# New durations for matmuls, and a margin for the banks of the row maxima, in a hand-planned instruction order (attention and bilinear feed-forward on one core)

## The chip, the cores and the metric

The kernel runs on one core of a Trainium2 chip. The metric is device time in microseconds (us) of one execution; the time given for a kernel is the median of its runs. The core's engines run side by side, each in the order in which its instructions were written: TensorE (PE in the profile, with its weight loads apart as PEld), VectorE (DVE), ScalarE (ACT), GpSimd (POOL), and the queue of SyncE (SP), which here issues most DMA transfers. They wait for one another only through semaphores.

## What is computed

```python
xn = _layernorm(x)                          # x: 1 x 2048 x 576
q, k, v = split((xn @ wqkv), H=32, Dh=18)
p  = softmax(q k^T * 18 ** -0.5)            # 32 heads, 2048 x 2048 each
s  = concat_heads(p v) @ wo
h  = (xn @ w_gate) * (xn @ w_up)            # 2048 x 4608
g  = silu(h @ w_down)                       # 2048 x 576
return x + s * g
```

Everything is float32. The two branches, attention `s` and the feed-forward (GLU) `g`, need only `xn`, and so they can run at the same time.

## The kernel before

**Three parts.** A prologue (about the first 195 us of the profiled execution) normalises x, makes q, k and v and writes them to DRAM. The main phase runs attention and the feed-forward together. An end part multiplies by `wo`, gates and stores.

**Two streams on TensorE.** A contraction in the main phase is cut to 64 rows, so a matmul uses half of the array's rows: rows 0 to 63 or rows 64 to 127. Stream `r = 0` is the sequence of matmuls on the lower half, `r = 1` that on the upper one, and two matmuls of different streams overlap. There are two lengths: 512 columns (`LONG`: the up and gate projections at L678, and both kinds of scores) and 288 columns (`SHORT`: the down projection at L720). The product of probabilities and values (`pv_group`, L639) uses all rows and so needs both streams to stop; such a pause is called a visit (`visit`), and one visit takes as a rule 7 tiles of 128 keys.

**The feed-forward** goes in 72 units. In each unit either stream makes two accumulations of 27 LONG matmuls (stream 0 the up projection, stream 1 the gate) and four of 12 SHORT ones. ACT copies the up result out (L683), DVE multiplies gate with up (L690), DVE adds each down result to its sums (`acc`, L748).

**Attention** computes the scores twice. An `a` item (`a_item`, L596 and L598) is a LONG matmul of scores for 128 queries and 512 keys and a maximum over its 512 columns on DVE (`mx`). When the 64 items of a head are done, `max_fold` and `max_rows` turn the maxima into two extra rows of the operands (`pair`). A `b` item (`b_item`, L628 and L630) is the same product transposed with the maximum already taken off, and an exponential on ACT (`pt`). There are 32 x 64 = 2048 items of each kind. In almost all of the main phase `a` items go on stream 0 and `b` items on stream 1. Four finished `b` items of one tile of keys are due for a visit.

**Banks.** PSUM has two banks for `a` results, two for `b` results, and four (`g`) that the up, gate, down and value products share. An `a` matmul must wait until DVE has read the maximum of the `a` item two before it.

**The planner.** `order()` (L1097 on) writes out the whole instruction order of the main phase before anything runs. It keeps a model of the time: `clk[r]` is the moment at which stream r can start its next matmul; `issue(r, length)` advances it by `length`; `engine(eng, start, taken)` keeps when DVE, ACT and POOL are next free; `banks[tag]` holds when each bank can be written again; `moved()` is the DMA queue. At each step the stream that is behind gets its next instruction: a score item if its bank is free by the model (`at <= clk[r]`) and its goal has come (`goal <= clk[r]`), else the next feed-forward matmul. Goals (`a_goal`, `b_goal`) spread the score items evenly over `span`, the planned length of the phase, which is worked out from LONG, SHORT and the length of the visits. The goals of the `a` items run ahead of an even spread by `SOONER` = 10 us at the end, and `b` item i has the goal of `a` item i + 88. `late()` holds an `a` item back when a feed-forward accumulation is about to end and needs DVE; it does so no longer when the item is 4 us behind its goal. For an `a` item the model gives DVE 0.60 us after the matmul's 0.456 us, adds 0.095 us (`TAIL`) and `EARLY` = 0.17 us, and then counts the bank as free.

The model's numbers change nothing but the order: which instruction stands before which on TensorE, and through it on the other engines. What is computed, how many instructions there are and what each costs stay as they are. Whatever the model says, the semaphores keep an instruction from running too early.

Of the kernel before, what the change touches and what calls it, by code (L numbers as in the profile page):

```python
# [40 lines left out]
def kernel(  # L41
# [536 lines left out]
    with ExitStack() as mid:  # L578
# [9 lines left out]
        def a_item(h, i, r=0):  # L588

            t, c = divmod(i, 4)  # L590
            if i == 0:
                mx[h] = gp.tile([128, NT, 4], FT, name="mx", bufs=1)
            q, k = (pairs[h % 2], ring) if r else (ring, pairs[h % 2])
            p = bank("a", 2)
            rows = slice(64 * r, 64 * r + 64)
            nc.tensor.matmul(p, q[rows, t * 128:(t + 1) * 128], k[rows, c * 512:(c + 1) * 512],  # L596
                             start=True, stop=True)
            nc.vector.tensor_reduce(mx[h][:, t, c:c + 1], p, axis=AX.X, op=OP.max)  # L598
# [3 lines left out]
        def max_fold(h):  # L602
            ms[h] = mp.tile([128, NT], FT, name="m", bufs=1)
            nc.vector.tensor_reduce(ms[h], mx.pop(h), axis=AX.X, op=OP.max)

        def max_rows(h):
            m = ms.pop(h)
            mm = mp.tile([128, 2, NT], FR, name="mm", bufs=1)
            mt = mp.tile([128, 32], FT, name="mt", bufs=1)
            nc.vector.tensor_scalar(mm[:, 0, :], m, -1.0, None, op0=OP.mult)  # L610
            nc.vector.scalar_tensor_tensor(mm[:, 1, :], m, -1.0, mm[:, 0, :].bitcast(FT),
                                           op0=OP.mult, op1=OP.subtract)
            nc.vector.transpose(mt, mm.rearrange("p a t -> p (a t)").bitcast(FT))  # L613
            for r in (64, 0) if h == H - 1 else (64,):
                q = ring if r == 0 else pairs[h % 2]
                for g in range(4):
                    rows = q[r + R:r + R + 2, :].rearrange("j (t g i) -> j g t i", g=4, i=32)[:, g].bitcast(FT)
                    nc.gpsimd.dma_start(rows, mt[32 * g:32 * g + 32, :])  # L618
# [224 lines left out]
            xi[t] = fin["ep"].tile([128, D], FT, name="xi", bufs=8)  # L843
            nc.sync.dma_start(xi[t], x2[rows, :])

        LONG, SHORT = 0.2335, 0.1335

        def stream(r):

# [38 lines left out]
        N = 64  # L888
        TOTAL = H * N
        LEAD, MOST = 24, 40  # L890
        EARLY = 0.17
        PACE, SKEW, PULL, FIRST, ROWS = 1.005, 3.0, 3.0, 2.0, 6.0
        slots, gone = [0, 0], [0.0, 0.0]
        clk, free = [0.0, 0.0], {"DVE": 0.0, "ACT": 0.0, "POOL": 0.0}
# [2 lines left out]
        banks = {"a": [0.0] * 2, "b": [0.0] * 2, "g": [0.0] * 4}  # L897
        turn = {"a": 0, "b": 0}

        def next_free(tag):  # L900
            if tag == "g":
                return min(banks["g"])
            return banks[tag][turn[tag] % len(banks[tag])]

        def engine(eng, start, taken):
            free[eng] = max(free[eng], start) + taken
            return free[eng] + TAIL[eng]

        def issue(r, length):

            at = issued[0] = max(clk[r], issued[0])
            clk[r] = at + length + (0.11 if fresh[r] else 0.0)
            fresh[r] = False
            return at + (0.456 if length == LONG else 0.356)
# [34 lines left out]
        def feed(r, h, i):  # L949

            if i == 0:
                if h:
                    stacks.append((load_ring, (r, h, 1)))
                if h + 1 < H and (r or h):
                    stacks.append((load_pair, (r, h + 1)))
            if i == 32 and h + 1 < H:
                stacks.append((load_ring, (r, h + 1, 0)))
            for at, want in ((10, (load_ring, (r, h, 1))), (48, (load_pair, (r, h + 1))), (52, (load_ring, (r, h + 1, 0)))):
                if i == at and want in stacks:
                    stacks.remove(want)  # L960
                    send(want, max(clk))

        def a_next(r=0):
            nonlocal na
            h, i = divmod(na, N)
            feed(0, h, i)
            a_item(h, i, r)
            slot = turn["a"] % 2
            turn["a"] += 1
            banks["a"][slot] = engine("DVE", issue(r, LONG), 0.60) + EARLY  # L970
            na += 1
            if i == N - 1:
                max_fold(h)
                max_rows(h)
                rows_done[h] = engine("DVE", 0.0, 0.85) + ROWS
# [5 lines left out]
        def b_next(r=1):  # L981
# [8 lines left out]
            end = engine("ACT", issue(r, LONG), 0.495)  # L990
            banks["b"][slot] = end + EARLY
            nb += 1
# [36 lines left out]
        def visit(now):  # L1029
# [4 lines left out]
            if due:  # L1034
                now = max(now, next_free("g") - EARLY + 0.03)
            for h, t, at in due:
# [5 lines left out]
            for h in sorted({h for h, _, _ in due[:many]}):  # L1042
                ts = [t for g, t, _ in due[:many] if g == h]
                now = max(now, next_free("g") - EARLY + 0.03) + 0.859 * len(ts)
                k = banks["g"].index(next_free("g"))
                pv_group(h, ts, k)
                end = engine("DVE", now + 0.25, 0.60) if ts[0] else engine("ACT", max(now + 0.25, shown[0]), 0.495)
                banks["g"][k] = end + EARLY
                if ts[-1] == NT - 1:
# [47 lines left out]
        def order():  # L1097
# [5 lines left out]
            while any(heads) or na < TOTAL or nb < TOTAL or due:  # L1103
# [20 lines left out]
                if r == 0 and (na < TOTAL or nb < TOTAL - N) or r == 1 and nb == 0 and na < N:  # L1124
                    at, goal, score, can = next_free("a"), a_goal(na) + lean, a_next, na < TOTAL and na < nb + N + MOST and stacked(0, na)
                    can = can and not late(goal, r)
                else:
                    at, goal, score, can = next_free("b"), b_goal(nb) + lean, b_next, b_ready(r)
# [9 lines left out]
                elif op is not None:  # L1138
# [8 lines left out]
                    if end:  # L1147
                        done = engine(end[0], lands, end[1])
                        banks["g"][slots[r]] = done + EARLY
                        if kind == "d":  # L1150
# [148 lines left out]
```

## Time and profile before

| | |
|---|---|
| median of 3 runs | 2575.25 us (2573.8 to 2578.24) |
| the profiled execution | 2576.35 us, of which the span is 2574.6 us |
| main phase, first up or gate matmul to the last visit's start | 194.8 to 2499.56 us |
| TensorE clock granted over the span | 1.000 |
| PE, DVE, ACT, POOL busy (share of the span) | 99%, 74%, 57%, 23% |

The span runs from the first to the last instruction; the 1.75 us beside it lie before and after. Busy time on PE is the time in which at least one matmul is on record as running. As two streams overlap and the ends of matmuls are modelled, a busy PE can still be losing time: whether it does is seen from the distance between the starts of one stream's matmuls.

### The profile page before, as it was taken

The page shows a single profiled execution, that of the slowest core. Times are in us where ns is not written, and L with a number is a line of the kernel's source. Part 1 is how long each engine was busy: PE and PEld are TensorE (multiplying, and loading weights), DVE is VectorE, ACT ScalarE, POOL GpSimd, SP SyncE. Part 2 cuts the span into 40 slices and gives each one's busy share as a digit, 9 for nine tenths or more (in the row PEclk, how much of TensorE's full clock was granted, in tenths as well). Part 3 has the DMA queues.
Part 4 walks back from the last instruction along what each step waited for, and adds up shares of the span by engine and source line. Part 5 has one row for each costly group of instructions (what it writes and reads, how often), then busy time and mean ns, then how long its engine had stood idle before and what let it go on. Part 6 is the DMA issues. An engine that isn't in the chain of part 4 may idle for free.

```text
span 2574.6 us, 59106 instructions
## 1 busy us (share of the span) xinstructions
PE 2558.4 (99%) x24360; PEld 2080.9 (81%) x24360; DVE 1917.3 (74%) x3377; ACT 1458.4 (57%) x2688; POOL 594.3 (23%) x663
## 2 busy tenths in 40 slices
PE   8999999999999999999999999999999999999999
PEld 7899887778878778877877788877787888887779
DVE  6209777778778888877788888877788888777527
ACT  5222666666655555655555565655555665555561
POOL 3214434434421111111111112111111211111125
PEclk9999999999999999999999999999999999999999
DMA  7799988887785666665686656656686666665567
GB/s 245 234 281 275 273 228 232 225 222 218 220 202 180 179 181 178 171 183 153 179 196 177 172 161 191 178 157 177 169 198 156 177 187 174 174 178 166 155 182 254
DMA packets 195897, 504.57 MB, mean 196 GB/s; under 512 B 58112, under 2 KB 116352, under 8 KB 156588
## 3 DMA queue, kind: packets, MB, share of 16 engines
q1 hardware_dynamic: 185676, 489.05, 67.9%
q0 software_dynamic: 9952, 11.74, 1.7%
q8 instruction: 192, 3.15, 0.6%
q14 instruction: 77, 0.63, 0.1%
HBM read 312.21 MB, written 107.61 MB: 163 GB/s over the span
## 4 chain that ended last, share of the span: by engine, by line
PE 98%; DVE 1%; DMA 1%; ACT 0%; issue 0%; SPq 0%
PE pg L678 35%; PE pg L639 17%; PE pg L720 16%; PE pa L596 11%; PE pb L628 9%; PE pg L402 2%; PE pa L348 2%; PE pb L348 2%; PE pg L1229 1%; PE pa L1229 1%; PE pb L1229 1%; DMA xc<-sx 0%; DMA xin<-in_A_x_dram 0%; PE pg L334 0%; DVE mx L598 0%; DVE xcx L338 0%
## 5 line engine op out<-in xcount | busy, mean ns | idle before, releaser
L598 DVE TENSOR_REDUCE mx<-pa 128x1 f32<-128x512 f32 x2048 | 1361.8, 685 | 150.2 <-PE pa L596 67.4
L630 ACT ACTIVATE pt<-pb 128x512 f32<-128x512 f32 x2048 | 1155.0, 598 | 549.0 <-PE pb L628 464.7
L678 PE MATMUL pg<-xc,wgu 64*128 64x512 f32 x7776 | 1381.0, 389 | 1.5 <-DMA xc<-sx 1.5
L678 PEld LDWEIGHTS pg<-xc,wgu 64*128 64x128 f32 x7776 | 1032.3, 184 | 54.7 <-DMA xc<-sx 3.1
L628 PE MATMUL pb<-pair,ring 64*128 64x512 f32 x2006 | 783.8, 397 | 0.5 <-ACT us L683 0.5
L596 PE MATMUL pa<-pair,ring 64*128 64x512 f32 x2001 | 781.1, 396 | 0.4 <-DVE mx L598 0.4
L720 PE MATMUL pg<-wd,hs 64*128 64x288 f32 x3408 | 531.3, 292 | 1.2 <-DVE acc L748 1.2
L720 PE MATMUL pg<-wd,hx 64*128 64x288 f32 x3408 | 524.6, 292 | 0.0
L720 PEld LDWEIGHTS pg<-wd,hs 64*128 64x128 f32 x3408 | 468.3, 185 | 6.6 <-DVE acc L748 1.9
L720 PEld LDWEIGHTS pg<-wd,hx 64*128 64x128 f32 x3408 | 462.7, 185 | 3.6 <-DMA hx<-hs 0.5
L639 PE MATMUL pg<-pt,vt 128*32 128x512 f32 x4096 | 454.8, 594 | 0.0
L694 POOL TENSOR_TENSOR hs<-us,hs 128x512 fp32r<-128x512 f32 x144 | 186.1, 1292 | 1120.3 <-ACT hs L693 1101.8
L596 PEld LDWEIGHTS pa<-pair,ring 64*128 64x128 f32 x2001 | 362.6, 184 | 92.0 <-issue 47.8
L628 PEld LDWEIGHTS pb<-pair,ring 64*128 64x128 f32 x2006 | 364.0, 184 | 11.3 <-ACT pt L630 1.4
L639 PEld LDWEIGHTS pg<-pt,vt 128*32 128x32 f32 x4096 | 125.5, 110 | 283.8 <-issue 280.7
L645 DVE TENSOR_TENSOR oc<-oc,pg 128x512 f32<-128x512 f32 x69 | 47.5, 688 | 319.2 <-PE pg L639 319.0
L748 DVE TENSOR_TENSOR acc<-acc,pg 128x288 f32<-128x288 f32 x544 | 234.6, 445 | 26.7 <-PE pg L720 24.0
L693 ACT ACTIVATE hs<-us 128x512 fp32r<-128x512 f32 x144 | 91.0, 632 | 155.8 <-DVE us L690 151.7
L659 POOL DMA_DIRECT2D sot<-oc x124 | 64.0, 523 | 327.7 <-DVE oc L656 325.4
L618 POOL DMA_DIRECT2D pair<-mt x128 | 78.0, 615 | 225.2 <-DVE mt L613 218.6
L643 ACT ACTIVATE oc<-pg 128x512 f32<-128x512 f32 x32 | 19.2, 599 | 189.3 <-PE pg L639 189.3
L194 POOL TENSOR_TENSOR wgu<-wraw,wgu 128x384 fp32r<-128x384 f32 x108 | 108.4, 1017 | 68.2 <-ACT wgu L193 47.8
(141 smaller groups left out, 1381.9 us busy)
## 6 DMA issues: line engine op xcount, KB each, us to landing
wgu<-swg SPq DMA_DIRECT2D x102, 1152.0 KB
hx<-hs SPq DMA_DIRECT2D x142, 512.0 KB
wd<-swd SPq DMA_DIRECT2D x50, 1152.0 KB
swg<-wgu SPq DMA_DIRECT2D x36, 1152.0 KB
pair<-sqk SPq DMA_DIRECT2D x192, 144.0 KB
ring<-sqk SPq DMA_DIRECT2D x384, 72.0 KB
swd<-wd SPq DMA_DIRECT2D x18, 1152.0 KB
sqk<-hl SPq DMA_DIRECT2D x32, 512.0 KB
```

Of the source, the lines that this page charges most:

```text
L194: nc.gpsimd.tensor_tensor(w[:, 9 + b:12 + b, :], raw[:, b:b + 3, :], w[:, b:b + 3, :].bitcast(FT), op=OP.subtract)
L348: nc.tensor.matmul(p, wq[b, a], xcs[c][:, e, :], start=n == 0, stop=n == len(PAIRS) - 1)
L596: nc.tensor.matmul(p, q[rows, t * 128:(t + 1) * 128], k[rows, c * 512:(c + 1) * 512], start=True, stop=True)
L598: nc.vector.tensor_reduce(mx[h][:, t, c:c + 1], p, axis=AX.X, op=OP.max)
L628: nc.tensor.matmul(p, k[rows, t * 128:(t + 1) * 128], q[rows, c * 512:(c + 1) * 512], start=True, stop=True)
L630: nc.scalar.activation(pt[t, c], p, AF.Exp, scale=scale)
L639: nc.tensor.matmul(p[32 * c:32 * c + 32, :], vt[h // 2][:, t, 6 * (h % 2):6 * (h % 2) + 32], pt[t, c], start=t == ts[0], stop=t == ts[-1])
L678: nc.tensor.matmul(ps, gw[n][half[r], a, :], xg[i][half[r], e, :], start=k == 0, stop=k == len(TERMS) - 1)
L693: nc.scalar.activation(hj[:, 0, :], h32, AF.Copy)
L694: nc.gpsimd.tensor_tensor(hj[:, 1, :], h32, hj[:, 0, :].bitcast(FT), op=OP.subtract)
L720: nc.tensor.matmul(ps[:, 0:HALF], (hx if k else hs)[u][half[r], j, a, s * 128:(s + 1) * 128], dw[u][half[r], k, j, e, :], start=n == 0, st ...
L748: nc.vector.tensor_tensor(a, a, ps[:, 0:HALF], op=OP.add)
```

## The change

Three numbers of the model change, all in the scope of the planner:

```diff
-        LONG, SHORT = 0.2335, 0.1335
+        LONG, SHORT = 0.2285, 0.1325
...
-        EARLY = 0.17
+        EARLY, LOAD = 0.17, 0.10
...
-            banks["a"][slot] = engine("DVE", issue(r, LONG), 0.60) + EARLY
+            banks["a"][slot] = engine("DVE", issue(r, LONG), 0.60) + EARLY + LOAD
```

A LONG matmul is counted 5 ns shorter, a SHORT one 1 ns shorter. `LONG` and `SHORT` also enter `part`, and with it `span` and `pace`, so the goals in model time move closer together. A bank of the maxima is taken to be usable 0.10 us later than before. The durations of DVE, ACT, POOL, DMA transfers and visits in the model stay.

## The prediction

> **What bounds the kernel now.** I read the page first (engines, then the chain that ended last), then the groups by line of the main phase, then two single stretches between visits.
>
> ```profile
> span 2574.6 us, 59106 instructions
> ...
> PE 2558.4 (99%) x24360; PEld 2080.9 (81%) x24360; DVE 1917.3 (74%) x3377; ACT 1458.4 (57%) x2688; POOL 594.3 (23%) x663
> ...
> PE 98%; DVE 1%; DMA 1%; ACT 0%; issue 0%; SPq 0%
> ```
>
> TensorE is 98% of the chain. The change neither adds nor removes an instruction, so the only time it can win is what TensorE loses between its matmuls. That amount comes from the groups by line of the main phase (window 194.7 to 2499.7):
>
> ```profile
> L678 PE MATMUL pg<-xc,wgu 64*128 64x512 f32 x7776 | 1381.0, 389 | 1.5 <-DMA xc<-sx 1.5
> L628 PE MATMUL pb<-pair,ring 64*128 64x512 f32 x2006 | 783.8, 397 | 0.5 <-ACT us L683 0.5
> L596 PE MATMUL pa<-pair,ring 64*128 64x512 f32 x2001 | 781.1, 396 | 0.4 <-DVE mx L598 0.4
> L720 PE MATMUL pg<-wd,hs 64*128 64x288 f32 x3408 | 531.3, 292 | 1.2 <-DVE acc L748 1.2
> L720 PE MATMUL pg<-wd,hx 64*128 64x288 f32 x3408 | 524.6, 292 | 0.0
> L639 PE MATMUL pg<-pt,vt 128*32 128x512 f32 x4068 | 451.8, 594 | 0.0
> L596 PE MATMUL pa<-ring,pair 64*128 64x512 f32 x47 | 18.7, 401 | 0.0
> L628 PE MATMUL pb<-ring,pair 64*128 64x512 f32 x42 | 16.9, 402 | 0.0
> ```
>
> and from the ends of the phase and one visit (one line's instructions, the timeline, the chain by pieces):
>
> ```profile
> L678 PE MATMUL pg<-xc,wgu x7776: 383/386/501, 194.8 to 2490.4; 64*128 64x512 f32 x200
> ...
> L596 PE MATMUL pa<-pair,ring x2001: 383/390/502, 200.6 to 2417.7; 64*128 64x512 f32 x182
> ...
> 2499.13 0.49 PE L628 MATMUL pb<-pair,ring 64*128 64x512 f32 x1
> 2499.56 2.78 PE L639 MATMUL pg<-pt,vt 128*32 128x512 f32 x24
> ...
> 358.37 6.15 PE pg L639 x56
> ...
> 387.91 6.15 PE pg L639 x56
> ```
>
> LONG matmuls: 7776 + 2006 + 2001 + 47 + 42 = 11872, or 5936 a stream. SHORT: 6816, or 3408 a stream. Visits: 4064 records before the last one (4068 less the 4 at its start) at 6.15 us for 56 give 446 us. With the new constants the work is 5936 x 0.2285 + 3408 x 0.1325 + 446 = 1356 + 452 + 446 = 2254 us; the phase took 2499.56 - 194.8 = 2305. So 51 us lie beyond the counted work, over some 74 stretches 0.69 us each. Not all of it can go. The stretch from 364.52 (end of a visit) to 387.91 is a clean one:
>
> ```profile
> L678 PE MATMUL pg<-xc,wgu 64*128 64x512 f32 x92 | 16.1, 389 | 0.0
> L596 PE MATMUL pa<-pair,ring 64*128 64x512 f32 x27 | 10.5, 395 | 0.0
> L628 PE MATMUL pb<-pair,ring 64*128 64x512 f32 x27 | 10.5, 394 | 0.0
> L720 PE MATMUL pg<-wd,hs 64*128 64x288 f32 x48 | 6.8, 292 | 0.0
> L720 PE MATMUL pg<-wd,hx 64*128 64x288 f32 x48 | 6.2, 292 | 0.0
> ```
>
> 146 LONG and 96 SHORT: 73 x 0.2285 + 48 x 0.1325 = 23.04 us against 23.39, a rest of 0.35 for starting and stopping. 74 such rests are 26 us. **A perfect order would win 51 - 26 = 25 us, 1%**; that is the ceiling. (The old constants give 23.45 for this stretch, more than it took: they held some of the stalls.) Part of the 25 us belongs to DMA:
>
> ```profile
> 730.00:758.00 28.00, 25.95 (x254) 22.25 (x254) 23.51 (x43) 18.84 (x35) 7.89 (x8) 1.00 0.98 212
> ```
>
> Here, where the next chunk of x is awaited (L678's 1.5 us above), 2.05 us of PE are empty, with the DMA engines 98% busy. The change touches no transfer.
>
> **The margin LOAD, what it removes.** The waits between engines, and the timeline of weight loads and matmuls around one of them:
>
> ```profile
> PEld pa L596 <- DVE mx L598: 8.3, 40, 0.9
> ...
> PE pa L596 <- DVE mx L598: 0.4, 1, 0.4
> ```
>
> ```profile
> 1500.40 0.39 PE L628 MATMUL pb<-pair,ring 64*128 64x512 f32 x1
> 1500.56 0.18 PEld L596 LDWEIGHTS pa<-pair,ring 64*128 64x128 f32 x1 [0.20 <-DVE mx L598]
> 1500.56 0.29 PEld L678 LDWEIGHTS pg<-xc,wgu 64*128 64x128 f32 x2
> ...
> 1500.63 0.42 PE L596 MATMUL pa<-pair,ring 64*128 64x512 f32 x1
> ...
> 1500.90 0.39 PE L628 MATMUL pb<-pair,ring 64*128 64x512 f32 x1
> ```
>
> The weight load of an `a` matmul waits for the bank, not the matmul. It takes 0.18 us, and while it waits the loads behind it wait too: L678's start at the same 1500.56. But the matmuls hardly notice: on stream 1 they start at 1500.40, then one slot later, then at 1500.90, so two slots took 0.50 us where 0.46 is usual (below). Some 0.04 us were lost for a hold of 0.20. Bounds for all: 0.4 us (PE's own row) and 8.3 us (every hold lost in full); 8.3 x 0.04/0.20 = 1.7. Shorter holds than the view lists (0.15 us) come on top. I take **-3 us**.
>
> **LONG and SHORT, what they move.** Of one stream's matmuls the model now sees 73 x 0.005 + 48 x 0.001 = 0.41 us less in a stretch, and everything else (goals, visits) in proportion. 28 `a` items a stretch stay 28, as `span` shrinks with the work. The two lengths now stand as 0.2285 to 0.1325, by 1.4% nearer to each other, so over a half stretch (12 us) in which one stream has SHORT and the other LONG work the model's two clocks shift by up to 0.17 us: bounds -74 x 0.17 = -13 us and +13 us, as nothing in the trace tells which pair fits that stretch better; nearest is the clean stretch, which the new pair meets after its 0.35. I take **-1 us**.
>
> **What the margin adds.** DVE's timeline shows a chain of `a` items, and the same at the end of its stretch:
>
> ```profile
> 1315.46 6.87 DVE L598 TENSOR_REDUCE mx<-pa 128x1 f32<-128x512 f32 x10
> ...
> 1334.21 0.69 DVE L598 TENSOR_REDUCE mx<-pa 128x1 f32<-128x512 f32 x1 [0.21 <-PE pa L596]
> 1335.34 0.69 DVE L598 TENSOR_REDUCE mx<-pa 128x1 f32<-128x512 f32 x1 [0.44 <-PE pa L596]
> 1336.47 0.69 DVE L598 TENSOR_REDUCE mx<-pa 128x1 f32<-128x512 f32 x1 [0.44 <-PE pa L596]
> ```
>
> Ten maxima in 6.87 us start (6.87 - 0.69)/9 = 0.69 us apart: three slots of 0.23. That is the bank limit of the model: 0.456 + 0.60 + 0.095 + 0.17 = 1.32 us for two items on two banks, rounded up to 6 slots. With LOAD it is 1.42; 6 slots of 0.2285 are 1.37, too short, so **two items take 7 slots**, 0.80 us each. Later, at 1334 to 1336, items come 1.13 us apart, DVE idle: there the goal paces them. So `a` items are late after each visit, catch up at 0.69, then wait for their goals. With 0.80 catching up takes longer. Half of 28 items in such clean chains cost 14 x 0.115 = 1.6 us; the others, amid sums and feed-forward ends on DVE, perhaps 0.4: together 2.0 us a stretch. The cover: six paced items at 1.1 that could come at 0.8, or 1.8 us. The account is about even, and `late()` lets go of an item 4 us behind, which frees more. If 0.2 us a stretch are lacking, `a` items end 74 x 0.2 = 15 us later than 2417.7. The last head's 64 `b` items need some 64 x 0.69 + 2.3 x 6.15 + 6.9 (the model's wait for the rows) = 65 us before 2499.56, so `a` items may end at 2434, 17 us later, before the end moves. I take **0 us**; if the cover is gone, see the first rival. Behind a held-back `a` item nothing waits on PE, since the planner puts a feed-forward matmul in its place.
>
> **Sum.** 2576.35 (the profiled execution) - 3 - 1 + 0 = 2572.35. That execution was 1.1 us above the median, so the forecast for the median is **2571.3 us**.
>
> **Rivals.**
>
> *The maxima fall behind: slower.* Speaks for it:
>
> ```profile
> 1497.50:1521.00 23.50, 23.50 (x240) 20.91 (x236) 23.18 (x42) 16.86 (x31) 5.04 (x6) 1.00 0.78 226
> 1521.00:1527.30 6.30, 6.30 (x60) 1.84 (x60) 1.05 (x3) 0.00 (x0) 0.00 (x0) 1.00 0.15 38
> ```
>
> Between visits DVE is busy 23.18 of 23.50 us, in the visit 1.05 of 6.30: it has no room there. 28 items in 23.5 us are 0.84 each, and 0.80 leaves 0.04 x 28 = 1.1 us for all that interrupts them. Against it: the paced items above and `late()`. It decides from a lack of more than 17/74 = 0.23 us a stretch. At 0.6 to 1.0 us, attention is 44 to 74 us late, 27 to 57 beyond the cover, or 0.9 to 1.9 stretches, and these run at the end without feed-forward work: 28 x 0.69 + 6.15 = 25.5 us where PE needs 28 x 0.2285 + 6.15 = 12.5. Price 13 us a stretch: +12 to +25, so 2583 to 2596. Chance 0.27.
>
> *Nothing that counts.* The holds are covered anyway and other waits take their turn: 2575. The row at 1500.56 allows it (0.04 us lost). [...] Chance 0.16.
>
> *More of the 25 us goes*, as the margin loosens the whole order and a chunk's wait falls otherwise: -12 us, 2563. The clean stretch shows that 0.35 can be had. Chance 0.14.
>
> **Chances and range.** The forecast's own case has 0.43, its range 2565 to 2577. A measurement of this kernel can tell 0.2%, 5.2 us: 2570.1 and 2580.4. Faster: 0.20 of the forecast, 0.01 of the second rival, the third's 0.14, 0.35 together. Same: 0.23 + 0.13 and 0.02 of the first rival, 0.38. Slower: 0.25 of the first and 0.02 of the second rival, 0.27. The range takes in the first rival's two prices and the third's 2563 with 3 us to spare: 2560 to 2596.
>
> **What would show it.** Right: PEld's row for `pa` falls below 4 us; chains of maxima at 0.80 instead of 0.69; the last L596 between 2410 and 2434; PE idle only at the chunk. Wrong: the last L596 beyond 2434, with PE rows at the end thin of L678 (first rival); the phase as long as before with PEld's row small (second). What would break the sum is DMA: another order of loads can make or mend stalls of 2 us each.

## The result: 3% slower, and the profile after

| | before | changed |
|---|---|---|
| median, beside each other | 2574.72 us (5 runs) | 2652.76 us (2647.0 to 2659.97, 5 runs) |
| ratio | | 1.0298, 95% interval 1.0279 to 1.0317 |
| profiled execution, span | 2576.35, 2574.6 us | 2647.0, 2645.1 us |
| last `a` matmul (L596) | 2417.7 | 2494.5 |
| last visit begins | 2499.56 | 2567.61 |

The forecast was 2571.3 us with a range up to 2596, and it was wrong: the change costs 78 us. The page of the changed kernel, its engines and its chain:

```profile
PE 2570.5 (97%) x24360; PEld 2115.3 (80%) x24360; DVE 1917.4 (72%) x3377; ACT 1462.1 (55%) x2688; POOL 594.6 (22%) x663
...
PE 87%; DMA 7%; DVE 4%; POOL 1%; issue 1%; ACT 0%; SPq 0%; ACTq 0%; POOLq 0%
```

The same work is done (the counts are those of before), but TensorE's share of the chain that ended last fell from 98 to 87%, and DMA took 7%. The groups by line of the main phase of the changed kernel say where:

```profile
L628 PE MATMUL pb<-pair,ring 64*128 64x512 f32 x2009 | 787.9, 399 | 48.3 <-DMA pair<-mt 37.3 <-DMA ring<-sqk 9.0 <-issue 1.9
L596 PE MATMUL pa<-pair,ring 64*128 64x512 f32 x2004 | 783.0, 396 | 1.7 <-DVE mx L598 1.5
```

Behind the bar stands the idle time of PE just before the line's matmuls: 0.5 us before, 48.3 us now, in front of `b` matmuls. 37.3 us of it end with a DMA `pair<-mt`. That is the transfer in `max_rows` (L618) which writes a head's negated maxima into the rows of `pair` that the `b` matmuls of that head read. One such wait, from the timeline of the changed kernel (POOL's idle time in brackets is no cost):

```profile
1107.61 0.21 DVE L613 STREAM_TRANSPOSE mt<-mm 128x32 f32<-128x32 f32 x1
...
1108.12 1.27 POOL L618 DMA_DIRECT2D pair<-mt  x2 [12.88 <-DVE mt L613]
...
1111.46 1.19 POOL L618 DMA_DIRECT2D pair<-mt  x2 [2.07 <-issue]
...
1113.73 0.39 PE L596 MATMUL pa<-pair,ring 64*128 64x512 f32 x1
1120.93 0.76 PE L628 MATMUL pb<-pair,ring 64*128 64x512 f32 x1 [6.81 <-DMA pair<-mt]
```

The transpose of the maxima ends at 1107.82; the four transfers are issued until 1112.65; the first `b` matmul that reads the rows starts at 1120.93. That is 13.1 us, where the model counts `ROWS` = 6. The planner believed the rows to be there, put the first `b` matmul of the next head into the order, and PE, which takes its instructions in turn, stood from 1114.1 on, with feed-forward work written behind it. DVE followed it: its next maximum came at 1123. The windows around the wait; a row has the length of the stretch, then the busy time of PE, PEld, DVE, ACT and POOL, and ends with the granted clock, the DMA share and GB/s:

```profile
1105.40:1113.70 8.30, 8.30 (x76) 6.81 (x74) 7.25 (x15) 6.63 (x12) 2.46 (x4) 1.00 0.71 186
1113.70:1120.90 7.20, 0.42 (x4) 0.01 (x1) 1.17 (x2) 0.00 (x0) 0.00 (x0) 0.75 0.58 102
1120.90:1128.00 7.10, 7.07 (x51) 6.13 (x53) 4.04 (x7) 3.96 (x8) 1.29 (x1) 0.77 0.37 132
1128.00:1138.60 10.60, 10.60 (x130) 10.28 (x126) 10.40 (x20) 7.06 (x13) 1.29 (x1) 1.00 0.73 246
```

The granted clock was 1.00 ahead of the wait, 0.75 over the stretch with it and 0.77 over the 7.1 us after it: 0.23 x 7.1 = 1.6 us more, by estimate. Two stretches of this kernel with the same work, 160 LONG and 89 SHORT matmuls each, give the whole price of a wait. First the groups by line on PE in the one with the wait, the rows with most time:

```profile
L678 PE MATMUL pg<-xc,wgu 64*128 64x512 f32 x104 | 21.7, 414 | 0.0
L628 PE MATMUL pb<-pair,ring 64*128 64x512 f32 x28 | 11.6, 420 | 6.8 <-DMA pair<-mt 6.8
```

The stretches begin and end at the transposed products of L639; in the chain of waits by pieces (start, length, what):

```profile
1099.38 6.22 PE pg L639 x56
...
1138.63 6.18 PE pg L639 x56
...
1169.35 2.76 PE pg L639 x21
```

The first, with the wait, runs from 1099.38 + 6.22 = 1105.60 to 1138.63, 33.0 us; the second from 1144.81 to 1169.35, 24.5 us. The wait of 6.8 us cost 8.5. Over the second stretch the granted clock was 1.00, and its L678 matmuls took 387 ns at the mean against the 414 above.

The main phase is 2567.61 - 195.2 = 2372.4 us long, 67.6 more than before; of the 70.5 us that the span grew, nearly all lie there. 48 us are the waits in front of L628. Of these, 9.0 us end not with the rows but with `ring<-sqk`, the transfer of the operands of the same `b` items, three times and each time before the first item of a head; why these came late was not followed. The granted clock was 0.989 over the span, 1.000 before, and by the estimate above, 1.6 us behind one wait, it accounts for a part of the remaining 20 us; I have not divided it exactly.

### The profile page after: what moved, and what is told of

It is laid out like the page before. It is cut to its first block, busy times and chain, and to the rows that moved or that the text cites. A ratio compares the mean times of both kernels' runs of the same rounds, so it can differ in the third digit from the quotient of the medians.

```text
span 2645.1 us, 59091 instructions
## 1 busy us (share of the span) xinstructions
PE 2570.5 (97%) x24360; PEld 2115.3 (80%) x24360; DVE 1917.4 (72%) x3377; ACT 1462.1 (55%) x2688; POOL 594.6 (22%) x663
## 4 chain that ended last, share of the span: by engine, by line
PE 87%; DMA 7%; DVE 4%; POOL 1%; issue 1%; ACT 0%; SPq 0%; ACTq 0%; POOLq 0%
PE pg L678 31%; PE pg L639 17%; PE pg L720 14%; PE pa L596 10%; PE pb L628 9%; DMA pair<-mt 3%; PE pg L402 2%; PE pb L348 1%; PE pa L348 1%; DVE mx L598 1%; DMA ring<-sqk 1%; PE pg L1229 1%; DMA hx<-hs 1%; POOL pair L618 1%; DMA sqk<-hl 1%
## 5 line engine op out<-in xcount | busy, mean ns | idle before, releaser
L678 PE MATMUL pg<-xc,wgu 64*128 64x512 f32 x7776 | 1462.1, 390 | 1.0 <-DMA xc<-sx 1.0
L678 PEld LDWEIGHTS pg<-xc,wgu 64*128 64x128 f32 x7776 | 1095.7, 186 | 50.4 <-DMA xc<-sx 1.9
L628 PE MATMUL pb<-pair,ring 64*128 64x512 f32 x2009 | 787.9, 399 | 48.3 <-DMA pair<-mt 37.3
L596 PE MATMUL pa<-pair,ring 64*128 64x512 f32 x2004 | 783.0, 396 | 1.7 <-DVE mx L598 1.5
L720 PE MATMUL pg<-wd,hs 64*128 64x288 f32 x3408 | 550.8, 294 | 2.1 <-DVE acc L748 1.6
L720 PE MATMUL pg<-wd,hx 64*128 64x288 f32 x3408 | 538.7, 293 | 4.0 <-DMA hx<-hs 4.0
L720 PEld LDWEIGHTS pg<-wd,hs 64*128 64x128 f32 x3408 | 482.6, 186 | 7.6 <-DVE acc L748 2.5
L720 PEld LDWEIGHTS pg<-wd,hx 64*128 64x128 f32 x3408 | 471.5, 186 | 8.2 <-DMA hx<-hs 4.6
L639 PE MATMUL pg<-pt,vt 128*32 128x512 f32 x4096 | 454.8, 594 | 0.4 <-DVE acc L748 0.2
L596 PEld LDWEIGHTS pa<-pair,ring 64*128 64x128 f32 x2004 | 367.6, 186 | 71.0 <-issue 46.9
L628 PEld LDWEIGHTS pb<-pair,ring 64*128 64x128 f32 x2009 | 368.0, 186 | 62.7 <-issue 51.6
L639 PEld LDWEIGHTS pg<-pt,vt 128*32 128x32 f32 x4096 | 125.5, 110 | 284.7 <-issue 281.1
L618 POOL DMA_DIRECT2D pair<-mt x128 | 78.0, 615 | 237.4 <-DVE mt L613 229.5
```

The source lines that it names most:

```text
L628: nc.tensor.matmul(p, k[rows, t * 128:(t + 1) * 128], q[rows, c * 512:(c + 1) * 512], start=True, stop=True)
L639: nc.tensor.matmul(p[32 * c:32 * c + 32, :], vt[h // 2][:, t, 6 * (h % 2):6 * (h % 2) + 32], pt[t, c], start=t == ts[0], stop=t == ts[-1])
L678: nc.tensor.matmul(ps, gw[n][half[r], a, :], xg[i][half[r], e, :], start=k == 0, stop=k == len(TERMS) - 1)
L720: nc.tensor.matmul(ps[:, 0:HALF], (hx if k else hs)[u][half[r], j, a, s * 128:(s + 1) * 128], dw[u][half[r], k, j, e, :], start=n == 0, st ...
```

## The experiments

Each kernel ran on the same chip as the kernel before, beside it (2576 to 2577 us there). The **theory**: with LOAD two maxima take seven slots instead of six, so the maxima lag; the `b` items come up against rows that take longer than the model's 6 us; PE waits. The **rival**: the new lengths spoil the order of the two streams.

| kernel | median us | ratio, 95% interval | last L596 | PE waits for pair<-mt |
|---|---|---|---|---|
| changed | 2652.76 | 1.0298 (1.0279 to 1.0317) | 2494.5 | 37.3 us, 9 times |
| e1, LOAD alone | 2605.01 | 1.0105 (1.0086 to 1.0124) | 2433.9 | 10.1 us, 4 |
| e2, lengths alone | 2583.98 | 1.0027 (1.0018 to 1.0037) | 2411.2 | none |
| e3, lengths, LOAD 0.05 | 2589.48 | 1.0043 (1.0028 to 1.0058) | 2413.5 | none |
| e4, changed, ROWS 12 | 2600.14 | 1.0088 (1.0073 to 1.0104) | 2437.8 | none |
| e5, before, LOAD 0.08 | 2575.98 | 0.9998 (0.9988 to 1.0007) | 2414.0 | none |
| e6, before, ROWS 12 | 2576.82 | 1.0000 (0.9991 to 1.0009) | 2418.3 | none |
| e7, middle lengths, LOAD 0.10 | 2624.55 | 1.0182 (1.0160 to 1.0204) | 2466.4 | 18.5 us, 5 |
| e8, before, LEAD 12 | 2652.61 | 1.0296 (1.0280 to 1.0313) | 2489.0 | 39.3 us, 10 |
| e9, longer lengths | 2578.35 | 1.0008 (0.9999 to 1.0017) | 2418.2 | none |

### e1, e2: each part alone

Both are edits of the changed kernel; e1 is the first pair of lines, e2 the second.

```diff
-        LONG, SHORT = 0.2285, 0.1325
+        LONG, SHORT = 0.2335, 0.1335
...
-        EARLY, LOAD = 0.17, 0.10
+        EARLY, LOAD = 0.17, 0.0
```

> The changed kernel with LONG and SHORT put back (0.2335, 0.1335), LOAD = 0.10 kept. Theory (the margin tips a rounding: two maxima on two banks take 1.411 us after the planner's tolerance of 0.01, six slots of 0.2335 are 1.401, so they take seven; the maxima lag, the rows for the next head come after the b matmuls that need them, and PE stands still): chains of maxima 0.80 us apart, last L596 at 2460 to 2500, several waits of PE at L628 for the DMA pair<-mt, time 2615 to 2660. Rival (the shorter LONG and SHORT spoil the order of the two streams, the margin is harmless): last L596 within 2410 to 2434, time 2565 to 2585.

> The changed kernel with LOAD = 0. Theory (rounding): 1.311 us are under six slots of 0.2285 (1.371), so chains stay at 0.69 us, the last L596 at 2410 to 2425, no wait of PE for pair<-mt, time 2565 to 2582. Rival (the lengths are the cause): 2640 to 2660, with the waits for pair<-mt.

Neither part alone does it. LOAD alone costs 28 us, less than the theory asked for, and the maxima end 16 us late, not 40 to 80. The lengths alone cost 7 us with no wait for the rows; that is 2 us above the theory's range and far from the rival's 2640. Together they cost 76 to 78, more than 28 + 7. So the theory was right on the kind of loss and incomplete on its cause; e7 asks what the lengths add. That LOAD tips the rounding is in DVE's timeline; first the changed kernel, where two maxima start 1.56 and 1.59 us after the two before (seven slots of 0.23 are 1.61), then e1, where it is 1.58, then e2, where ten start (6.87 - 0.69)/9 = 0.69 us apart:

```profile
1148.32 1.35 DVE L598 TENSOR_REDUCE mx<-pa 128x1 f32<-128x512 f32 x2
1149.88 1.37 DVE L598 TENSOR_REDUCE mx<-pa 128x1 f32<-128x512 f32 x2 [0.22 <-PE pb L628]
1151.47 1.37 DVE L598 TENSOR_REDUCE mx<-pa 128x1 f32<-128x512 f32 x2 [0.21 <-PE pg L678]
```

```profile
1108.82 1.37 DVE L598 TENSOR_REDUCE mx<-pa 128x1 f32<-128x512 f32 x2 [0.17 <-PE pa L596]
1110.40 1.37 DVE L598 TENSOR_REDUCE mx<-pa 128x1 f32<-128x512 f32 x2 [0.21 <-PE pa L596]
```

```profile
1499.35 6.87 DVE L598 TENSOR_REDUCE mx<-pa 128x1 f32<-128x512 f32 x10
```

The page of the kernel before gives the mean time of one maximum, the number behind the comma:

```profile
L598 DVE TENSOR_REDUCE mx<-pa 128x1 f32<-128x512 f32 x2048 | 1361.8, 685 | 150.2 <-PE pa L596 67.4
```

A maximum takes DVE 0.685 us itself, so starts 0.69 us apart mean that DVE has no idle time; that spacing alone, from which the prediction read the bank limit of the model, could as well be DVE's own pace. What tells the two apart is the idle time of some 0.2 us after each pair with LOAD = 0.10.

Of e1's 28 us, 10.1 are waits for the rows. PE's other waits in its main phase come to 17.5 us, against 3.6 in the kernel before, in small pieces that end with several engines and transfers; they were not followed.

For the 7 us of e2 the waits of PE give a hint. They are in the end part, at the products with `wo`:

```profile
PE pa L1229 <- DVE ys L1238: 2.2, 1, 2.2
...
PE pa L1229 <- ACT hi L822: 1.9, 1, 1.9
```

In the profile of the kernel before PE has no wait at L1229. So 4 of the 7 us arise after the main phase. What in the order brings them was not tried.

### e3, e5: is it the size of the margin or the rounding?

e3 is the changed kernel with the first pair of lines, e5 the kernel before with the rest.

```diff
-        EARLY, LOAD = 0.17, 0.10
+        EARLY, LOAD = 0.17, 0.05
...
-        EARLY = 0.17
+        EARLY, LOAD = 0.17, 0.08
...
-            banks["a"][slot] = engine("DVE", issue(r, LONG), 0.60) + EARLY
+            banks["a"][slot] = engine("DVE", issue(r, LONG), 0.60) + EARLY + LOAD
```

> The changed kernel with LOAD = 0.05 in place of 0.10. Theory (rounding): 1.361 us are still under 1.371, so nothing of the cost is left: chains at 0.69 us, time 2565 to 2582. Rival (the cost grows with the margin, half the margin half the cost): last L596 near 2455, time 2600 to 2625.

> The kernel before (LONG, SHORT = 0.2335, 0.1335) with LOAD = 0.08. Theory (rounding to slots): 1.391 us are under six slots of 0.2335 (1.401), where 0.10 was over (1.411) and cost 28 us with these lengths; so chains of maxima stay at 0.69 us, the last L596 comes at 2410 to 2428, time 2568 to 2584. Rival (the cost grows with the margin): 0.8 of the 28 us, 2593 to 2603.

e5 is the clean test. With the old lengths 0.08 costs nothing (ratio 0.9998) and 0.10 costs 28 us (e1): 20 ns of margin decide, because they tip two maxima from six slots into seven. With these lengths a cost in step with the margin is excluded. DVE's timeline of e5 has its chain unchanged, ten maxima (6.84 - 0.69)/9 = 0.68 us apart:

```profile
1499.18 6.84 DVE L598 TENSOR_REDUCE mx<-pa 128x1 f32<-128x512 f32 x10
```

e3 missed its range by 7 us: the big loss is gone and no wait for `pair<-mt` is left, but against e2 0.05 us of margin went with another 5.5 us. In the profiled executions PE's waits in the main phase come to 12 us in e3 and 7 in e2, and the largest difference is a wait of 2.9 us for the transfer `hx<-hs` at L720 (0.2 in e2). Why that one comes with the margin was not found, so with the new lengths a small cost below the rounding is not excluded.

e5 also answers what the held weight loads were worth. PEld's waits of e5:

```profile
PEld pa L596 <- DVE mx L598: 5.6, 12, 1.3
```

28 of the 40 holds are gone (8.3 us of holding before, 5.6 now) and the time is the same. They cost PE nothing that can be measured here; the interval of e5 reaches from -3 to +2 us, so a gain of 1 us would not be seen.

### e7, e9: what the lengths add

e7 is the changed kernel with the first pair of lines, e9 the kernel before with the second.

```diff
-        LONG, SHORT = 0.2285, 0.1325
+        LONG, SHORT = 0.2310, 0.1330
...
-        LONG, SHORT = 0.2335, 0.1335
+        LONG, SHORT = 0.2360, 0.1345
```

> The changed kernel with LONG, SHORT = 0.2310, 0.1330, half way between old and new, LOAD = 0.10. Seven slots for two maxima in all three. Theory (a shorter slot leaves DVE, whose 0.60 us stay, less time a stretch in the model, so the lag grows steadily with it): last L596 between the 2434 of the old and the 2494 of the new lengths, 2445 to 2480, time 2615 to 2640. Rival (the new lengths do harm by something else that comes at once): 2595 to 2610 or 2645 and more.

> The kernel before with LONG, SHORT = 0.2360, 0.1345, the lengths moved the other way; no LOAD. Theory (lengths act through the time that the model leaves DVE): chains still at six slots, 0.69 us; DVE gets more time a stretch in the model, so the maxima keep their goals, no wait of PE for pair<-mt; the goals in model time lie further apart, so that the last L596 comes later than 2418 by some 5 to 15 us; time 2565 to 2585, faster than before only if the end part gains by it. Rival (the better the model's lengths fit the trace's 0.23, the faster the kernel): slower than the kernel before, in step with the 7 us that the shorter lengths cost, 2580 to 2590.

With LOAD = 0.10 and seven slots throughout, the time rises with the shortening of the lengths: 2605, 2625, 2653, and so do the last L596 (2434, 2466, 2494) and the waits for the rows (10.1, 18.5, 37.3 us). This bears the theory out: the model's DVE still needs 0.60 us for a maximum while a stretch has become 0.41 us shorter, so in the model less time is left for 28 maxima. It fits, and the lag is in the order itself, before anything runs: by the planner's own clock in `order()`, the `a` items of the last four heads stand on average 20, 29 and 31 us behind their goals in these three kernels, and 7 in the kernel before, e2 and e3. That DVE's time is the link was argued from the planner's arithmetic and not isolated. Without LOAD, lengths moved the other way cost nothing (e9): its interval reaches from 0.9999 to 1.0017. The rival that the lengths that fit best are fastest fell with it, as did a part of the expectation, for the last L596 stayed at 2418.

### e4, e6: the time to the rows

e4 is the changed kernel with these edits, e6 the kernel before with the same. The second edit only moves two fetches of `o`, the attention output that `wo` multiplies, behind the loads that are left when the main phase ends.

```diff
-        PACE, SKEW, PULL, FIRST, ROWS = 1.005, 3.0, 3.0, 2.0, 6.0
+        PACE, SKEW, PULL, FIRST, ROWS = 1.005, 3.0, 3.0, 2.0, 12.0
...
+    for f, a, _ in loads:
+        f(*a)
     for k in (3, 4):
         fetch_o(k, 0)
-    for f, a, _ in loads:
-        f(*a)
```

> The changed kernel with the model's time from the maxima to the usable rows, ROWS, at 12 in place of 6 us, and, in the end part, the pending loads and stores issued ahead of the loads of the last two parts of o. Theory (most of the loss is PE waiting for rows that the model takes to be there): the waits of PE for pair<-mt fall from 37 us to under 5, chains of maxima stay at 0.80 us, the last L596 at 2430 to 2455, time 2580 to 2610. Rival (the waits for the rows are a symptom, the slower maxima cost the time wherever they are waited for): time 2635 to 2660, with the lost time in other waits or at the end of the main phase.

> The kernel before with ROWS = 12 and with the pending loads and stores of the end part issued ahead of the loads of the last two parts of o, the same two edits that brought the changed kernel from 2653 to 2600 us. Theory (they win only where b items had caught up with the rows): the first b item of a head stood 12 to 22 us behind its rows anyway, so the time is 2568 to 2584. Rival (the two edits win or cost by themselves, whatever the change does): under 2565 or over 2590.

Told that the rows take 12 us, the planner writes feed-forward matmuls in place of the `b` items: no wait for `pair<-mt` is left, and 52 of the 76 us return, while the chains keep seven slots. The same edits in the kernel before change nothing (1.0000), so they have no value of their own. Of the 23 us that remain, a part is the loss that the prediction's first rival described, attention that runs without feed-forward work at the end. One line's instructions in e4:

```profile
L628 PE MATMUL pb<-pair,ring x2006: 383/388/792, 262.8 to 2514.6; 64*128 64x512 f32 x183
...
L678 PE MATMUL pg<-xc,wgu x7776: 383/386/503, 194.4 to 2479.4; 64*128 64x512 f32 x200
```

The last L678 starts at 2479.4, but the down projection (L720) goes on to 2502.0, and the last `b` matmul starts at 2514.6: some 13 us without feed-forward work. Before the change the last `b` matmul (2499.13) came ahead of the end of L720 (2510.5). The granted clock was 0.997 over e4's span of 2596.4 us, 1.000 before, which makes 0.003 x 2596.4 = 8 us by estimate. The longest `b` matmul took 792 ns, the longest of L678 503, which speaks for a low clock behind the last L678. The rest of the 23 us was not divided.

### e8: late rows without slower maxima

One line of the kernel before:

```diff
-        LEAD, MOST = 24, 40
+        LEAD, MOST = 12, 40
```

> The kernel before with LEAD = 12 in place of 24, so that b items follow the a items 12 items (some 13 us) closer; lengths and banks as before. Theory (b matmuls that come before their rows stop PE, however fast the maxima are): chains stay at 0.69 us, the first b item of a head comes within 5 to 12 us of its rows, PE waits at L628 for pair<-mt, some 20 us or more in all, time 2590 to 2650. Rival (without slower maxima the rows are in time): 2565 to 2584.

The `b` items are told to follow the `a` items 12 items closer, nothing else. From DVE's timeline and the waits of PE in e8:

```profile
425.94 5.51 DVE L598 TENSOR_REDUCE mx<-pa 128x1 f32<-128x512 f32 x8
```

```profile
PE pb L628 <- DMA pair<-mt: 39.3, 10, 9.8
```

Eight maxima (5.51 - 0.69)/7 = 0.69 us apart: the chain is as fast as before. And the time is 2652.6 us, 3 us above the expected range, with 39.3 us of waits: a loss as large as that of the changed kernel without its change (that the two agree to the microsecond is chance). So what costs the larger part of the time is the distance between a head's maxima and its first `b` matmul, however it shrinks. Neither the changed kernel nor any of these nine beats the one before.

## Why the prediction was wrong, step by step

**The cover of the maxima is the step that failed**: "`a` items may end at 2434, 17 us later, before the end moves. I take **0 us**". e1 puts the first half of it to the test: the prediction had the maxima end 15 us later, and with LOAD alone they ended 16 us later, at 2433.9, inside the 17 us. Yet e1 lost 28 us. The cover had been looked for in one place, the end of the phase, and with the model's own wait for the rows (6.9 us) in the sum. The cover that ran out lies at every change of head. Counted in the trace, the first `b` matmul of a head started 12.3 to 22.4 us after the end of the head's transpose (L613) before the change; in the changed kernel from the tenth head on 5.8 to 13.1 us, and where PE waited for the rows 8.0 to 13.1 had gone by. The time to the rows varies: counted in the same way, the last of a head's four transfers landed 3.9 to 13.0 us after the transpose in the kernel before, 8.0 at the median and in 21 of 32 heads after more than 6. The kernel before never felt that the model's 6 us were too short, as its `b` items came late enough. It was in its trace all the same: the four transfers are issued over some 3 us after the transpose, and the list of DMA issues of the kernel before gives the median time from issue to landing, the last number:

```profile
pair<-mt POOLq DMA_DIRECT2D x128, 4.0 KB, 5.5
```

Issue and landing together are beyond 6 us, and I took the planner's figure instead of adding them.

**"Everything else (goals, visits) in proportion" was wrong too.** "28 `a` items a stretch stay 28, as `span` shrinks with the work" holds for matmuls and goals and not for DVE, whose 0.60 us a maximum stay. The lengths alone cost 7 us where the prediction had a gain of 1, and made LOAD's 28 us into 76 (e1, e7, changed). That DVE's unchanged time does this is the reading that fits, not one that an experiment isolates, and 4 of the 7 us lie in the end part.

**LOAD's gain** of 3 us is not seen: e5 has 28 of the 40 holds fewer and the same time. The row at 1500.56 had said 0.04 us a hold, or 1.1 us for the 28; so small a gain is within the interval and stays open.

**Right** were the rounding to seven slots (0.80 us seen as 1.56 to 1.59 a pair), the lag of the maxima that it causes, and the direction and the first half of the first rival. The 23 us that e4 shows once the waits are taken out lie within its price of 12 to 25 us, but in e4 only some 13 us ran without feed-forward work, so that agreement is in part luck. The larger part, 52 us, was no term of any case. Behind a held-back `a` item indeed little waits on PE (1.7 us in front of L596 in the changed kernel). The ceiling of 25 us was not put to the test, and it bounds gains only: nothing bounded the loss, and the range drew its upper end from one place where it could arise.

**The chance** of 0.27 for slower was too small for another reason: the account of 2.0 us lost against 1.8 us of cover stood on an edge, and no case counted the time in which PE would stand. In the changed kernel the last L596 is 77 us late, where e1's is 16. The order explains some 20 of the 77 us (e4, without waits for the rows, has it 20 us late), and most of the rest is PE standing: e8 has its last L596 71 us late with maxima as fast as before. As the order is fixed beforehand, a wait moves the maxima and the `b` items behind it alike; it is the order that brings a head's `b` items close to its rows.

## What to carry to other kernels

In an order written out ahead, each wait that the model takes for granted (here the landing of a head's rows, 3.9 to 13.0 us after the transpose in the kernel before, where the model counts 6) is only as good as the slack that has so far hidden it: before slack is spent, measure that wait in the trace and not in the model. Margins in a model that works in slots act in steps; work out how many slots a chain takes before and after, and how far the next step is. And when one engine's durations are rescaled, ask which durations were left, since the ratio between engines moves even where the total seems to scale.

## What the runs showed of the hardware beyond the forecast

A transfer of 4 KB issued on POOL's queue took 5.5 us at the median from issue to landing in the kernel before and 6.6 us in the changed one, with the packets of one queue taking 68% and 66% of the 16 DMA engines' time over the span. From the transpose of the maxima to the first matmul on the rows 13.1 us went by in the changed kernel's longest case. A wait of PE of 6.8 us cost 8.5 us. The granted clock was 1.00 from 1113.7 to 1117.3 us, with PE idle for all but the first 0.4 us of it, and 0.50 from 1117.3 to 1124.1. Of these 6.8 us 3.2 lie behind the end of the wait, which lose 0.50 x 3.2 = 1.6 us by estimate. The LONG matmuls in those 3.2 us took 610 to 625 ns at the mean, line by line; in the second stretch, at a granted clock of 1.00, they took 387 to 392.
